# Top-k attention with two gated layers behind it: plain float32 output weights for the first chunk, one bank for rows of two batches, a later start of the W2 conversion

## Chip, cores and metric

The kernel runs on one core of one Trainium2 chip. Its time is the device time of one execution in microseconds (us), lower is better. TensorE is called PE here, VectorE DVE, ScalarE ACT, GpSimd POOL, SyncE SP, as in the profile; the DMAs are issued by SP, in the order of its part of the program.

## The reference

```python
# attention: q, k, v are (4, 8, 576, 64)
scores = matmul(q, k.T) / sqrt(64)
kth    = 32nd largest score of the row
attn   = softmax(where(scores >= kth, scores, -1e9))
x      = (attn @ v) as (2304, 512)
# first layer, weights 512 -> 1536 -> 512
x = (silu(x @ w_gate) * (x @ w_val)) @ w_out
# second layer, weights 512 -> 2048 -> 512
h = x @ w_in
out = (h * cos(h)) @ w2_out
```

The weights come as float64, and the kernel makes float32 of their words itself.

## The kernel before, in words

2304 tokens are 18 tiles of 128 rows. Two tiles are a *chunk* of 256 tokens, so there are nine chunks, 0 to 8. A *unit* is one tile and one head: 16 units make a chunk (four pairs of heads, two tiles, two heads), 144 units in all, in the order chunk, pair, tile, head. In a unit PE multiplies q by the 576 keys into one two-bank PSUM tile `sc` (four matmuls of 288 columns, line 549), ACT copies the scores out (`s`, line 555), DVE runs four MAX8 and three MATCH_REPLACE8 over them (lines 581 and 584) to find the 32 largest, POOL makes the bounds (lines 595, 599), ACT makes the kept exponentials (Prelu at 612, Exp at 623). For two units PE then transposes (645), and multiplies by V (683, 686). A sequence of a batch is 576 rows, four tiles and a half, so tile 4 and tile 13 hold rows of two batches. For their 16 units (eight in chunk 2, eight in chunk 6) `unit_proc` does the scores twice, once with the keys of each batch: it computes all 128 rows, copies the 64 that count, waits until `sc` is free, computes all rows with the other keys, and copies the other 64.

The first layer of a chunk follows one chunk later, in 12 steps f over the 1536 hidden columns, spread between the units of the next chunk: `gemm_proc` multiplies x by W1 (`gv`, line 817, 24 matmuls for each f), ACT and POOL make the gated product `vv`, ACT and POOL split it into two float32r parts `gh` and `gl` (851, 854), and `wout_proc` adds 12 matmuls of 256 columns to `y` (871): high weights by `gh`, high weights by `gl`, low weights by `gh`, for four blocks of output. Both factors are split into a float32r part and its rest.

The output weights `wo` are converted once, in the time of chunk 0's first layer, in 24 half blocks: `convert` is a load (`wr`), three ACT operations (216, 224, 220), one DVE join (261) and one POOL addition (230); `halve` then splits the float32 result with one ACT copy (275) and one POOL subtraction (279). `wo0_store_proc` writes each split block of 512 KB to DRAM (line 336), and `wo_proc` loads it again for each of the eight later chunks (line 368). Two buffers hold `wo` blocks. Early pieces of the second layer's weights W2 go through the same `convert`, 48 of them, and back to DRAM (`w2_early_proc`).

What sets the order: a planner (`Plan`) runs when the program is built, takes a cost for each step and a due time (`due_unit(u)` is u times 4.97), and writes one fixed sequence for each engine and for SP's DMA queue. On the chip every engine works its sequence off in that order and waits where something is not there. The second layer (lines 1080 to 1144) begins when the last chunk's first layer is nearly done.

## Time and profile before

| | |
|---|---|
| time, median of 3 runs | 1313.93 us (1313.81 to 1314.13) |
| the profiled execution's own time | 1311.49 us |
| its span, first to last instruction | 1309.7 us |
| mean granted clock of PE | 0.965 of full speed |
| busy: PE, DVE, ACT, POOL | 92%, 78%, 76%, 51% of the span |
| attention, with the first layer of the chunk before between | until 810.4 us, the end of the last MAX8 |
| second layer alone | the last 402.7 us |

An engine's busy time is the union of its instructions' spans, so a busy PE need not be issuing at its full rate. The rows below give the attention chunk by chunk. Such a stretch begins with the first MAX8 of the chunk's first unit and ends with that of the next chunk.

### The profile page before, as it was taken

The page shows a single profiled execution, that of the slowest core. Times are in us where ns is not written, and L with a number is a line of the kernel's source. Part 1 is how long each engine was busy: PE and PEld are TensorE (multiplying, and loading weights), DVE is VectorE, ACT ScalarE, POOL GpSimd, SP SyncE. Part 2 cuts the span into 40 slices and gives each one's busy share as a digit, 9 for nine tenths or more (in the row PEclk, how much of TensorE's full clock was granted, in tenths as well). Part 3 has the DMA queues.
Part 4 walks back from the last instruction along what each step waited for, and adds up shares of the span by engine and source line. Part 5 has one row for each costly group of instructions (what it writes and reads, how often), then busy time and mean ns, then how long its engine had stood idle before and what let it go on. Part 6 is the DMA issues. An engine that isn't in the chain of part 4 may idle for free.

```text
span 1309.7 us, 25255 instructions
## 1 busy us (share of the span) xinstructions
PE 1205.0 (92%) x8704; PEld 1115.2 (85%) x8704; DVE 1018.0 (78%) x2040; ACT 990.6 (76%) x2308; POOL 668.5 (51%) x1111
## 2 busy tenths in 40 slices
PE   3567789799999999999999999987999999999998
PEld 2356678799999999989999999987899999999997
DVE  7998998899999999988999997336655555555554
ACT  7998899998988988899888887548655545555554
POOL 5865888776678776676767665767210000000000
PEclk9866899999999999999999999998999999999999
DMA  6642244564546654555544432574010100000000
GB/s 216 194 126 78 70 142 166 178 190 154 168 141 184 184 177 147 161 151 188 167 142 156 136 119 89 196 249 160 28 43 7 39 11 26 23 11 27 1 25 25
DMA packets 85408, 153.69 MB, mean 117 GB/s; under 512 B 16416, under 2 KB 39456, under 8 KB 85280
## 3 DMA queue, kind: packets, MB, share of 16 engines
q1 hardware_dynamic: 85280, 152.08, 37.0%
q8 instruction: 68, 1.11, 0.3%
q14 instruction: 60, 0.49, 0.1%
HBM read 130.02 MB, written 22.02 MB: 116 GB/s over the span
## 4 chain that ended last, share of the span: by engine, by line
PE 49%; DVE 6%; ACT 6%; DMA 4%; POOL 3%; issue 2%; SPq 0%; POOLq 0%; ACTq 0%; DVEq 0%
PE o L1144 15%; PE h L1080 14%; PE gv L817 8%; PE y L871 5%; DVE m L581 2%; PE av L686 2%; DVE w L584 2%; PE sc L549 2%; PE tp L645 2%; DMA wr<-in_w 2%; DVE th L844 1%; POOL w L1016 1%; ACT s L555 1%; DMA wo<-wo 1%; PE av L683 1%
## 5 line engine op out<-in xcount | busy, mean ns | idle before, releaser
L817 PE MATMUL gv<-xh,w 128*128 128x256 f32 x1536 | 332.3, 295 | 7.6 <-ACT hg L784 7.5
L581 DVE MAX8 m<-w 128x8 f32<-128x576 f32 x432 | 307.9, 746 | 0.5
L817 PEld LDWEIGHTS gv<-xh,w 128*128 128x128 f32 x1536 | 259.5, 193 | 15.6 <-ACT hg L784 9.8
L817 PE MATMUL gv<-xl,w 128*128 128x256 f32 x768 | 218.1, 284 | 0.0
L584 DVE MATCH_REPLACE8 w<-m,w 128x576 f32<-128x576 f32 x288 | 212.1, 741 | 0.0
L1080 PE MATMUL h<-x2h,w 128*128 128x384 f32 x720 | 200.8, 340 | 4.2 <-DVE g L1114 4.0
L871 PE MATMUL y<-gh,wo 128*128 128x256 f32 x864 | 178.1, 289 | 6.9 <-ACT gh L851 3.6
L1144 PE MATMUL o<-w,gh 128*128 128x512 f32 x540 | 183.8, 395 | 0.0
L549 PE MATMUL sc<-K,q 128*128 128x288 f32 x640 | 131.6, 331 | 39.4 <-ACT s L555 26.6
L871 PEld LDWEIGHTS y<-gh,wo 128*128 128x128 f32 x864 | 144.0, 194 | 10.7 <-ACT gh L851 4.4
L1047 POOL TENSOR_TENSOR x2l<-x,x2h 128x384 fp32r<-128x384 f32 x24 | 25.7, 1070 | 244.3 <-ACT x2h L1036 244.3
L817 PEld LDWEIGHTS gv<-xl,w 128*128 128x128 f32 x768 | 147.9, 193 | 0.0
L549 PEld LDWEIGHTS sc<-K,q 128*128 128x128 f32 x640 | 100.8, 208 | 51.9 <-ACT s L555 26.8
L645 PE MATMUL tp<-ident,e 128*128 128x128 f32 x648 | 116.4, 292 | 30.1 <-ACT pt L650 27.4
L1114 DVE TENSOR_TENSOR g<-r,h 128x384 f32<-128x384 f32 x96 | 53.1, 554 | 116.7 <-ACT r L1109 116.7
L1080 PEld LDWEIGHTS h<-x2h,w 128*128 128x128 f32 x720 | 132.7, 189 | 9.0 <-DVE g L1114 5.1
L1107 ACT ACTIVATE r<-r 128x384 f32<-128x384 f32 x96 | 50.2, 525 | 109.7 <-DVE r L1104 109.7
L854 POOL TENSOR_TENSOR gl<-vv,gh 128x256 fp32r<-128x256 f32 x108 | 81.1, 751 | 95.1 <-ACT gh L851 63.3
L871 PE MATMUL y<-gl,wo 128*128 128x256 f32 x432 | 123.9, 287 | 1.5 <-POOL gl L854 1.3
L1080 PE MATMUL h<-x2l,w 128*128 128x384 f32 x360 | 121.8, 338 | 0.0
L555 ACT ACTIVATE s<-sc 128x576 f32<-128x576 f32 (+1 forms) x160 | 104.1, 651 | 21.9 <-PE sc L549 20.2
L581 DVE MAX8 m<-s 128x8 f32<-128x576 f32 x144 | 105.0, 744 | 17.1 <-ACT s L555 15.5
(109 smaller groups left out, 2955.4 us busy)
## 6 DMA issues: line engine op xcount, KB each, us to landing
wo<-wo SPq DMA_DIRECT2D x108, 512.0 KB, 3.6
w_raw<-in_w SPq DMA_DIRECT2D x24, 512.0 KB, 4.9
V<-in_vP SPq DMA_DIRECT2D x48, 256.0 KB, 2.9
wr<-in_w SPq DMA_DIRECT2D x48, 256.0 KB, 3.7
kx<-in_kT SPq DMA_DIRECT2D x64, 144.0 KB, 2.9
qx<-in_qT SPq DMA_DIRECT2D x70, 128.0 KB, 3.1
wr<-in_wo SPq DMA_DIRECT2D x24, 256.0 KB, 2.8
w2d<-cvx SPq DMA_DIRECT2D x48, 128.0 KB, 3.0
```

The source lines that it names most:

```text
L549: nc.tensor.matmul(sc[:, s, :HALF], q[:, a, t * 128:t * 128 + 128], k[:, s * HALF:s * HALF + HALF], start=a == 0, stop=a == 1)
L555: nc.scalar.activation(st["s"][r0:r1], sc[r0:r1, :, :HALF], AF.Copy)
L581: nc.vector.max(out=st["m"][:, 8 * i:8 * i + 8], in_=st["w"] if i else st["s"])
L584: nc.vector.match_replace(out=st["w"], in_to_replace=st["m"][:, 8 * i:8 * i + 8], in_values=st["w"] if i else st["s"], imm_value=LOWEST)
L645: nc.tensor.transpose(st["ps"][:, j - j0], e[:, j * 128:j * 128 + 128], ident)
L817: nc.tensor.matmul(gv[g], w[kk // 2][:, a, g, kk % 2], m[:, kk], start=kk == 0 and i == 0, stop=kk == KT - 1 and i == 2)
L854: end = yield "POOL", 0.69, lambda: nc.gpsimd.tensor_sub(G[c, f][1], vv, G[c, f][0]), due, True
L871: nc.tensor.matmul(y1p[d // 2][:, d % 2], w[:, a, d * 128:d * 128 + 128], m, start=f == 0 and i == 0 and d % 2 == 0, stop=f == NF1 - 1 and ...
L1080: nc.tensor.matmul(st["h"], w[:, a, kk * 128:kk * 128 + 128], m[:, kk], start=kk == 0 and n == 0, stop=kk == KT - 1 and n == 2)
L1107: yield "ACT", 0.41, lambda: nc.scalar.activation(r, r, AF.Abs), due, True
L1114: nc.vector.tensor_mul(st["g"], r, h)
L1144: nc.tensor.matmul(o[t], a[:, cs], W2[f, 1][:, m], start=f == 0 and n == 0, stop=f == NF2 - 1 and n == 2)
```

## The change

Three edits are made together.

- **Scores of two batches.** `unit_proc` issues the matmuls for both batches one behind the other, the second batch's keys for all 128 rows first, and then the first batch's for the rows 0 to 63 alone, into the same bank. One ACT copy of 128 rows follows. `sc` is freed once for each unit.
- **Chunk 0's output weights.** The POOL addition that ends `convert` writes float32 straight into the `wo` block, and nothing is split: chunk 0's `wout_proc` issues four float32 matmuls for each f (the unsplit weights by the unsplit `vv`) in place of 12 float32r ones, and `gemm_proc` returns for chunk 0 before the split into `gh` and `gl`. The block is stored as 256 KB to a new tensor `wo32`. In chunk 1 `wo_proc` loads those 256 KB, splits them with one ACT copy and one POOL subtraction of 512 columns, and stores the split block of 512 KB to `wo`, from which chunks 2 to 8 load as before. So 24 ACT copies and 24 POOL subtractions of 256 columns, and 12 pairs of `gh` and `gl`, go; 12 copies and 12 subtractions of 512 columns come, and 12 stores move from chunk 0's time to chunk 1's. There are 12 more DMAs in all (120 on `wo` blocks for 108).
- **W2.** The due time of the i-th early piece is `due_unit(46 + 1.9 * i)` and was `due_unit(38 + 2 * i)`.

```diff
@@ -261,7 +262,7 @@
         t = yield "DVE", 0.08 + 0.55 * wide, lambda: nc.vector.scalar_tensor_tensor(
             st["x"], high, 3, st["y"], op0=OP.logical_shift_left, op1=OP.bitwise_or), due, True
         r_cy.free(n, t, plan)
-        t = yield "POOL", 0.13 + 1.12 * wide, lambda: cv_pool(raw, st["x"]), due, True
+        t = yield "POOL", 0.13 + 1.12 * wide, lambda: cv_pool(raw, st["x"], (into or (lambda: st["x"]))()), due, True
         read(t)
 
     def halve(raw, tile_out, due, read, done):
...
@@ -322,19 +324,23 @@
         now = yield "DMA", 1.05, load, due - 4.0, True
         yield r_wo.gate(f)
 
-        def tile_out():
+        def into():
             if f not in WO:
-                WO[f] = moe.tile([128, 2, DM], F32R, tag="wo", name="wo", bufs=r_wo.n)
-            return WO[f][:, :, cs]
-
-        plan.start(halve(st["raw"], tile_out, due, lambda t: r_wr.free(i, t, plan),
-                           lambda t: ev_wo0[f].set(t, plan)), now)
+                WO[f] = moe.tile([128, 2, DM], F32, tag="wo", name="wo", bufs=r_wo.n)
+            return WO[f][:, 0, cs].bitcast(I32)
+
+        def read(t):
+            r_wr.free(i, t, plan)
+            r_cvx.free(st["n"], t, plan)
+            ev_wo0[f].set(t, plan)
+
+        plan.start(convert(st["raw"], due, read, st, into), now)
 
     def wo0_store_proc(f):
         yield ev_wo0[f]
         ev_wo[0, f].set(ev_wo0[f].time, plan)
-        t = yield "DMA", 2.1, lambda: nc.sync.dma_start(wo[f], WO[f].bitcast(F32)), moe_due(0, f), True
-        wo_stored[f].set(t, plan)
+        t = yield "DMA", 1.1, lambda: nc.sync.dma_start(wo32[f], WO[f][:, 0]), moe_due(0, f), True
+        wo_whole[f].set(t, plan)
         r_wo.free(f, t, plan)
 
 
...
@@ -342,7 +348,7 @@
 
     def w2_early_proc(i):
         f, q = divmod(i, 4)
-        due = due_unit(38 + 2 * i)
+        due = due_unit(46 + 1.9 * i)
         cs = slice(q * 256, q * 256 + 256)
         k = 2 * NF1 + i
         yield r_wr.gate(k)
...
@@ -360,15 +366,27 @@
 
     def wo_proc(c, f):
         k = c * NF1 + f
-        yield wo_stored[f]
+        yield wo_whole[f] if c == 1 else wo_stored[f]
         yield r_wo.gate(k)
+        due = moe_due(c, f)
 
         def load():
             WO[k] = moe.tile([128, 2, DM], F32R, tag="wo", name="wo", bufs=r_wo.n)
-            nc.sync.dma_start(WO[k].bitcast(F32), wo[f])
-
-        t = yield "DMA", 1.6, load, moe_due(c, f), True
+            if c == 1:
+                nc.sync.dma_start(WO[k][:, 1].bitcast(F32), wo32[f])
+            else:
+                nc.sync.dma_start(WO[k].bitcast(F32), wo[f])
+
+        t = yield "DMA", 1.1 if c == 1 else 1.6, load, due, True
+        if c == 1:
+            x = WO[k][:, 1].bitcast(F32)
+            yield "ACT", 0.52, lambda: nc.scalar.activation(WO[k][:, 0], x, AF.Copy), due, True
+            t = yield "POOL", 1.25, lambda: nc.gpsimd.tensor_sub(WO[k][:, 1], x, WO[k][:, 0]), due, True
         ev_wo[c, f].set(t, plan)
+        if c == 1:
+            t = yield "DMA", 2.1, lambda: nc.sync.dma_start(wo[f], WO[k].bitcast(F32)), due, True
+            wo_stored[f].set(t, plan)
+            r_wo.free(k, t, plan)
 
 
     K, Q, V = {}, {}, {}
...
@@ -530,7 +548,7 @@
     ev_av = {(c, p): Event(SIZES[c]) for c in range(NCH) for p in range(NP)}
     ev_sum = {(c, p): Event(2 * SIZES[c]) for c in range(NCH) for p in range(NP)}
     r_x, r_rs = Ring(2), Ring(1)
-    tp_count, sc_count = [0], [0]
+    tp_count = [0]
 
     def unit_proc(u):
         c, p, t, h = units[u]
...
@@ -543,29 +561,28 @@
         yield r_s.gate(u + 1)
         q = Q[c, p, h]
 
-        def qk(k):
-            for s in range(2):
-                for a in range(2):
-                    nc.tensor.matmul(sc[:, s, :HALF], q[:, a, t * 128:t * 128 + 128], k[:, s * HALF:s * HALF + HALF],
-                                     start=a == 0, stop=a == 1)
-
-        def copy(r0, r1):
-            if "s" not in st:
-                st["s"] = att.tile([128, 2, HALF], F32, tag="s", name="s", bufs=r_s.n)
-            nc.scalar.activation(st["s"][r0:r1], sc[r0:r1, :, :HALF], AF.Copy)
-
-
+        def qk():
+
+            for b, r0, r1 in segs[::-1]:
+                k = K[b, p, h]
+                for s in range(2):
+                    for a in range(2):
+                        nc.tensor.matmul(sc[:r1, s, :HALF], q[:, a, t * 128:t * 128 + r1],
+                                         k[:, s * HALF:s * HALF + HALF], start=a == 0, stop=a == 1)
+
+        def copy():
+            st["s"] = att.tile([128, 2, HALF], F32, tag="s", name="s", bufs=r_s.n)
+            nc.scalar.activation(st["s"], sc[:, :, :HALF], AF.Copy)
+
+        yield r_sc.gate(u)
+        end = yield "PE", 0.57 * len(segs), qk, due - SC_LEAD, True
         for b, r0, r1 in segs:
-            n = sc_count[0]
-            sc_count[0] += 1
-            yield r_sc.gate(n)
-            end = yield "PE", 0.57, lambda k=K[b, p, h]: qk(k), due - SC_LEAD, True
             if kb_last[b, p, h] == u:
                 r_k.free(kvis[b, p, h], end, plan)
-            if t == SIZES[c] - 1 and r1 == 128:
-                r_q.free((c * NP + p) * 2 + h, end, plan)
-            end = yield "ACT", 0.53, lambda r0=r0, r1=r1: copy(r0, r1), due - SC_LEAD + 1.0, True
-            r_sc.free(n, end, plan)
+        if t == SIZES[c] - 1:
+            r_q.free((c * NP + p) * 2 + h, end, plan)
+        end = yield "ACT", 0.53, copy, due - SC_LEAD + 1.0, True
+        r_sc.free(u, end, plan)
         st["s"] = st["s"].rearrange("p a b -> p (a b)")
         yield r_w.gate(u)
         yield r_m.gate(u)
...
@@ -844,6 +861,10 @@
         yield name, cost, lambda: eng.tensor_mul(th, th, hg), due, True
         end = yield name, cost, lambda: eng.tensor_mul(vv, th, vv), due, True
         r_th.free(k, end, plan)
+        if c == 0:
+            G[c, f] = vv
+            ev_g[c, f].set(end, plan)
+            return
         yield r_g.gate(k)
 
         def hi():
...
@@ -865,16 +886,22 @@
             yield ev_wo[c, f]
 
             def part(d, f=f, k=k):
+                w = WO[k]
+                if c == 0:
+                    nc.tensor.matmul(y1p[d // 2][:, d % 2], w[:, 0, d * 128:d * 128 + 128], G[c, f],
+                                     start=f == 0 and d % 2 == 0, stop=f == NF1 - 1, skip_group_check=True)
+                    return
                 gh, gl = G[c, f]
-                w = WO[k]
                 for i, (a, m) in enumerate(((0, gh), (0, gl), (1, gh))):
                     nc.tensor.matmul(y1p[d // 2][:, d % 2], w[:, a, d * 128:d * 128 + 128], m,
                                      start=f == 0 and i == 0 and d % 2 == 0, stop=f == NF1 - 1 and i == 2,
                                      skip_group_check=True)
 
             for d in range(KT):
-                end = yield "PE", 0.36, lambda d=d, part=part: part(d), due, False
+                end = yield "PE", 0.36 if c else 0.45, lambda d=d, part=part: part(d), due, False
             r_g.free(k, end, plan)
+            if c == 0:
+                r_vv.free(k, end, plan)
             r_wo.free(k, end, plan)
         due = moe_due(c, NF1)
         for d in range(KT):
```

What the planner makes of it, at three places. The names in the rows are the tiles of the program; the lines of the changed kernel are some 17 to 20 higher than before. First ACT near unit 33, one of the eight of chunk 2 with rows of two batches. Before, from the middle of a `convert` on:

```order
L224 ACTIVATE cvx<-wr 128x256
L220 ACTIVATE wr<-wr 128x256
L783 ACTIVATE th<-gv_98 128x256
L784 ACTIVATE hg<-gv_98 128x256
L851 ACTIVATE gh_2648<-vv 128x256
L731 ACTIVATE rs<-tp 128x256
L555 ACTIVATE s<-sc 64x576
L275 ACTIVATE wo<-cvx 128x256
L216 ACTIVATE wr<-wr 128x256
L224 ACTIVATE cvx<-wr 128x256
L220 ACTIVATE wr<-wr 128x256
L555 ACTIVATE s<-sc 64x576
```

and now, from that unit's Prelu on:

```order
L629 ACTIVATE e<-s,b_2417 128x576
L575 ACTIVATE s<-sc 128x576
L217 ACTIVATE wr<-wr 128x256
L225 ACTIVATE cvx<-wr 128x256
L221 ACTIVATE wr<-wr 128x256
L800 ACTIVATE th<-gv_99 128x256
L801 ACTIVATE hg<-gv_99 128x256
L748 ACTIVATE rs<-tp 128x256
L465 ACTIVATE K<-kx 128x576
L756 ACTIVATE rx<-av 128x256
L640 ACTIVATE e,sm<-e,b_2417 128x576
L217 ACTIVATE wr<-wr 128x256
```

The copies of 64 rows and of `wo<-cvx` are gone, and one copy of 128 rows (line 575) stands for two; the conversion's triples are still there. Second PE, where chunk 0 multiplies by its first output weights. Before:

```order
L817 MATMUL gv_98<-xh,w_2_360 128x256
L871 MATMUL y_100<-gh_1309,wo 128x256
L871 MATMUL y_100<-gl_1310,wo 128x256
L871 MATMUL y_100<-gh_1309,wo 128x256 x2
L871 MATMUL y_100<-gl_1310,wo 128x256
L871 MATMUL y_100<-gh_1309,wo 128x256
L871 MATMUL y_101<-gh_1309,wo 128x256
L871 MATMUL y_101<-gl_1310,wo 128x256
L871 MATMUL y_101<-gh_1309,wo 128x256 x2
L871 MATMUL y_101<-gl_1310,wo 128x256
```

and now:

```order
L570 MATMUL sc<-K,q 128x288 x4
L700 MATMUL av<-pt,vtail_106 128x128
L703 MATMUL av<-pt,V 64x128 x8
L891 MATMUL y_101<-vv,wo 128x256 x2
L891 MATMUL y_102<-vv,wo 128x256 x2
```

The twelve matmuls by `gh` and `gl` have become four by `vv`. Third SP's queue in the time of chunk 1's first layer. Before, loads of split blocks (line 368) only:

```order
L368 DMA wo<-wo 128x1024
L515 DMA V<-in_vP 128x512
L517 DMA vtail_104<-in_vP 64x64 x2
L368 DMA wo<-wo 128x1024
L488 DMA qx<-in_qT 64x2x256 x2
L357 DMA w2d<-cvx 128x256
L353 DMA wr<-in_w 128x256
L515 DMA V<-in_vP 128x512
L517 DMA vtail_105<-in_vP 64x64 x2
L368 DMA wo<-wo 128x1024
```

and now loads of whole blocks (line 376) and stores of split ones (line 387):

```order
L376 DMA wo<-wo_65 128x512 x2
L506 DMA qx<-in_qT 64x2x256 x2
L387 DMA wo<-wo 128x1024
L533 DMA V<-in_vP 128x512
L535 DMA vtail_106<-in_vP 64x64 x2
L387 DMA wo<-wo 128x1024
L458 DMA kx<-in_kT 64x576 x2
L376 DMA wo<-wo_65 128x512 x2
L506 DMA qx<-in_qT 64x2x256 x2
L387 DMA wo<-wo 128x1024 x2
L376 DMA wo<-wo_65 128x512
```

Loads and stores of `wo` alternate, and the pieces of W2 (lines 353 and 357 before) have moved behind. On DVE the early W2 pieces' joins stand behind units 38, 40 (two), 42, 44 and 45 in chunk 2 before, and behind units 44 and 47 now; the last stands behind unit 131 before and 134 now.

## Rows read from the trace of the kernel before

**Rows 1.** Busy time in stretches: length, PE, PEld, DVE, ACT, POOL (instructions), clock, DMA share, GB/s.
```profile
104.40:202.40 98.00, 77.58 (x549) 69.44 (x547) 90.77 (x189) 85.83 (x211) 77.83 (x123) 0.83 0.31 103
202.40:305.20 102.80, 91.86 (x805) 85.87 (x805) 90.17 (x180) 95.57 (x240) 79.70 (x137) 0.98 0.58 183
305.20:389.20 84.00, 83.92 (x760) 81.09 (x758) 83.67 (x183) 73.83 (x187) 56.49 (x106) 1.00 0.49 151
389.20:473.30 84.10, 81.52 (x719) 77.86 (x717) 81.56 (x178) 76.07 (x195) 64.61 (x115) 1.00 0.59 180
...
556.40:646.50 90.10, 87.71 (x793) 83.67 (x794) 81.71 (x175) 80.82 (x199) 65.67 (x118) 1.00 0.56 170
646.50:730.60 84.10, 83.42 (x763) 80.34 (x762) 83.16 (x180) 73.45 (x192) 55.19 (x107) 1.00 0.49 150
...
810.40:907.00 96.60, 83.72 (x650) 80.65 (x649) 38.36 (x46) 56.97 (x139) 64.13 (x75) 0.94 0.60 198
907.00:1309.70 402.70, 398.88 (x1988) 359.20 (x1986) 215.71 (x383) 220.95 (x431) 29.48 (x26) 1.00 0.08 25
```

**Rows 2.** Waits, 202.4 to 305.2 us: who for whom, us, times, longest.
```profile
DVE m L581 <- ACT s L555: 5.0, 7, 1.8
DVE cvx L261 <- ACT cvx L224: 4.2, 2, 2.6
```

**Rows 3.** Waits, 556.4 to 646.5 us.
```profile
DVE m L581 <- ACT s L555: 7.0, 2, 4.1
```

**Rows 4.** Timeline around 612 us, chunk 6: start, duration, instruction, idle before it.
```profile
609.77 0.39 PE L683 MATMUL av<-pt,vtail 128*128 128x128 f32 x2
...
612.41 0.28 PE L871 MATMUL y<-gl,wo 128*128 128x256 f32 x1
...
612.53 0.28 PE L871 MATMUL y<-gh,wo 128*128 128x256 f32 x1
...
612.65 0.70 PE L549 MATMUL sc<-K,q 128*128 128x288 f32 x4
...
613.39 0.64 ACT L555 ACTIVATE s<-sc 64x576 f32<-64x576 f32 x1 [0.66 <-PE sc L549]
...
614.70 0.70 PE L549 MATMUL sc<-K,q 128*128 128x288 f32 x4
...
615.88 0.65 ACT L555 ACTIVATE s<-sc 64x576 f32<-64x576 f32 x1
...
616.63 0.76 DVE L581 MAX8 m<-s 128x8 f32<-128x576 f32 x1 [4.10 <-ACT s L555]
```

**Rows 5.** Instructions by line and shape: busy us, mean ns, idle before.
```profile
L555 ACT ACTIVATE s<-sc 64x576 f32<-64x576 f32 x32 | 20.6, 643 | 4.0 <-PE sc L549 3.7
...
L279 POOL TENSOR_TENSOR w<-cvx,w 128x512 fp32r<-128x512 f32 x24 | 30.6, 1278 | 8.9 <-ACT w L275 8.5
...
L275 ACT ACTIVATE w<-cvx 128x512 fp32r<-128x512 f32 x24 | 14.9, 626 | 1.0 <-POOL cvx L230 0.9
```

**Rows 6.** Stretches, tile `wo` alone: length, PE, PEld, ACT, POOL.
```profile
104.40:202.40 98.00, 9.69 (x72) 9.11 (x72) 5.41 (x13) 9.59 (x13) 0.83 0.31 103
202.40:305.20 102.80, 22.45 (x156) 20.58 (x156) 4.56 (x11) 8.26 (x11) 0.98 0.58 183
```

**Rows 7.** Stretches, tile `gh` alone: length, PE, PEld, DVE, ACT, POOL.
```profile
104.40:202.40 98.00, 9.69 (x48) 7.96 (x48) 0.00 (x0) 2.98 (x7) 5.17 (x7) 0.83 0.31 103
202.40:305.20 102.80, 22.21 (x104) 17.80 (x104) 0.00 (x0) 5.08 (x12) 8.83 (x12) 0.98 0.58 183
```

**Rows 8.** Stretches, tile `wr` alone: length, DVE, ACT, POOL.
```profile
202.40:305.20 102.80, 11.29 (x16) 20.64 (x51) 12.39 (x17) 0.98 0.58 183
305.20:389.20 84.00, 3.21 (x8) 8.91 (x21) 5.23 (x7) 1.00 0.49 151
```

**Rows 9.** The page, DMA issues: KB each, median us to landing.
```profile
wo<-wo SPq DMA_DIRECT2D x108, 512.0 KB, 3.6
...
wr<-in_wo SPq DMA_DIRECT2D x24, 256.0 KB, 2.8
```

More of the change, by code (lines that the diff above doesn't have):

```diff
@@ L162, in topk_attention_moe_moe @@
     wo = dram.tile([NF1, 128, 2, DM], F32, name="wo")
+    wo32 = dram.tile([NF1, 128, DM], F32, name="wo32")
     w2d = dram.tile([NS2, 128, 2 * DM], F32, name="w2d")
@@ L227, in cv_join, with cv_pool @@
         nc.vector.scalar_tensor_tensor(x, cv_words(raw)[1], 3, y, op0=OP.logical_shift_left, op1=OP.bitwise_or)
-    def cv_pool(raw, x):
-        nc.gpsimd.tensor_tensor(x, x, cv_words(raw)[0], op=OP.add)
+    def cv_pool(raw, x, out):
+        nc.gpsimd.tensor_tensor(out, x, cv_words(raw)[0], op=OP.add)
     W1, WO = {}, {}
@@ L238, in topk_attention_moe_moe, with convert @@
     cv_count = [0]
-    for f in range(NF1):
+    for f in range(2 * NF1):
         r_wo.freed[f] = Event(2)
-    def convert(raw, due, read, st):
+    def convert(raw, due, read, st, into=None):
         low, high = cv_words(raw)
@@ L308, in topk_attention_moe_moe @@
     ev_wo0 = [Event(2) for _ in range(NF1)]
+    wo_whole = [Event() for _ in range(NF1)]
     def wo0_proc(i):
@@ L994, in w2_proc @@
             r_cy2.free(n, t, plan)
-            t = yield "POOL", 1.23, lambda: cv_pool(st["raw"], st["x"]), due, True
+            t = yield "POOL", 1.23, lambda: cv_pool(st["raw"], st["x"], st["x"]), due, True
             r_raw2.free(n, t, plan)
```

## The prediction

> **What bounds the kernel now.** I read the table of stretches first, chunk by chunk, then who waits for whom in the two stretches that stand out, and then the timeline of one such wait. Chunks 3, 4 and 7 take 84.0, 84.1 and 84.1 us for their 16 units, and DVE and PE are both busy for 97 to 100% of that [rows 1]. That is what 16 units cost when all goes well. Three stretches are longer: chunk 1, which I call A, with 98.0 us, chunk 2, which I call B, with 102.8, and chunk 6 with 90.1 [rows 1]. In B DVE is busy 90.2 us and PE 91.9 of 102.8, so neither of the two is full there; ACT is, with 95.6 us or 93%, where chunk 3 asks 73.8 of it [rows 1]. DVE waits in B for the score copies (5.0 us in 7 waits) and for the second ACT step of the conversions (4.2 us in 2) [rows 2]. In chunk 6 two waits of DVE for score copies make 7.0 us [rows 3], and the timeline shows how the longer one comes about: a copy of 64 rows ends at 614.03, PE issues the second batch's matmuls behind other work at 614.70, the second copy comes at 615.88, and MAX8 starts 4.10 us late [rows 4]. Behind the attention come 96.6 us of the last chunk's first layer and 402.7 us of the second layer alone, in which PE is busy 398.9 [rows 1]. The change does not reach into that; what the attention saves moves it forward as a whole, since each engine's sequence there hangs on the last chunk's x.
>
> **The change part by part.** A and B hold all of chunk 0's first layer: 13 and 11 of the 24 `wo` copies [rows 6], 7 and 5 of chunk 0's 12 `gh` (the 12 of B hold chunk 1's first 7) [rows 7].
>
> *ACT in A.* 13 `wo` copies (5.41 us) and 7 `gh` (2.98) go: 85.8 becomes 77.4. POOL loses 9.59 and 5.17: 77.8 becomes 63.1 [rows 1, 6, 7].
>
> *ACT in B.* Eight copies of 64 rows go (8 x 0.643 = 5.1) [rows 5], 11 `wo` copies (4.6) [rows 6] and five of twelve `gh` (2.1) [rows 7]. Four W2 pieces leave B, as DVE's order shows (six joins behind units 32 to 47 before, two now); 17 pieces took 20.64 us of ACT, so four take 4.9 [rows 8]. Ten of the twelve new copies of 512 columns stand there by ACT's order; the same form is the split of W1, 0.626 us each, so 6.3 come [rows 5]. Net: 95.6 - 5.1 - 4.6 - 2.1 - 4.9 + 6.3 = 85.2. POOL: 79.7 - 8.3 - 3.7 - 2.9 + 9 x 1.278 = 76.3 [rows 1, 5 to 8], well under B's length.
>
> *What that makes of the lengths.* Three bounds for B. ACT at today's share of 93% would need 85.2 / 0.93 = 91.6. DVE has four joins fewer at 11.29 / 16 = 0.71 [rows 8], so 87.4, and at the share of chunk 3 87.7. PE: chunk 6 has the same two-batch units and nearly the same count of matmuls (793 for 805), and was busy 87.7 [rows 1]; with a half of the extra below, 89.6. The longest of the three holds: B goes from 102.8 to 91.6, 11.2 less. A is bound by DVE: 90.8 busy, at chunk 3's share 91.1, and ACT at its present 87.6% would need 88.4. I put A at 92, 6.0 less. In chunk 6 the eight removed copies take away the second trip; PE, busy 87.7, is the bound, so 88.0, 2.1 less [rows 1].
>
> *What comes later.* Four W2 pieces now fall behind B. DVE is full there, so their joins count in full: 4 x 3.21 / 8 = 1.6 us more [rows 8]. Their ACT steps, and two new copies and three subtractions in chunk 3, lie beside DVE: ACT has 10 us free there and POOL 27 [rows 1]; without that cover ACT's 4.9 and these 5.1 us [rows 5] would come on top.
>
> *Plain float32 matmuls.* The trace has no 256-column one. The nearest row is line 683: one float32 matmul of 128 columns is two records, 0.39 us together where one record is 0.28 [rows 4], so 0.11 apart, 0.22 for 128 columns and 0.44 for 256. Three float32r ones of 256 take 3 x 0.12 = 0.36, from the starts at 612.41, 612.53 and 612.65 [rows 4]. 48 of them make 48 x 0.08 = 3.8 us more. Bounds: two records of 256 columns at 0.12 each would be 5.8 us less, and at half the clock the difference doubles to 7.7 us more. I take 3.8 us, since line 683 is the same kind of matmul. It lies in A and B, where PE has 20.4 and 10.9 us free [rows 1], so it costs nothing as long as PE does not become the bound.
>
> *Costs that I put at nothing.* The buffer `vv` is held until the matmuls instead of until `gl`; two stand ready. The extra 12 DMAs and the moved stores: the DMA share is 0.31 in A and 0.58 in B [rows 1]. What SP waits for is the third rival. Sum: -11.2 - 6.0 - 2.1 + 1.6 = -17.7. The profiled execution took 1311.5 (span 1309.7), the median of the runs is 1313.9, 2.4 above it, and I keep that distance: 1313.9 - 17.7 = 1296.2.
>
> **A rule that speaks against it.** DVE's joins read two tensors. They last 3.21 / 8 = 0.40 us in chunk 3 and 0.71 in B [rows 8], where POOL is busy 78% of the time and not 67% [rows 1]. The Trainium skill, in "SBUF — State Buffer", section "SBUF: two separate sides", says that a DVE operation with two SBUF inputs and a GpSimd operation that reads SBUF exclude each other for a whole instruction; by that rule the new wide subtractions hold DVE's joins off for longer than the halves did, and the longer joins of B agree with it. By the rows, such a subtraction lasts 1.278 us [rows 5]; behind units 36 to 47, where they stand, DVE has three joins left. Even if each met one in full, 3 x 1.28 = 3.8 us come on top, and the sum is -13.9. The joins beside them read 0.71 already, so I leave this out of the sum.
>
> **The rivals.** *First, PE binds.* If PE is the bound in A and B, since the plain matmuls come where its clock is half (the mean granted clock of A is 0.83 [rows 1]), their 7.7 us count in full, and with the blocked joins 3.8 more: -17.7 + 7.7 = -10.0 to -6.2, some 1304 to 1308. For it speaks that PE is full in every good chunk; against it the 31 us that it has free in A and B.
>
> *Second, only the copies help.* ACT's relief could be worth nothing, if what delays A and B is the chain from chunk to chunk and not ACT's load. Then DVE's waits for copies go (5.0 in B [rows 2], 2.1 in chunk 6) and the joins come: -5.5, so 1308.4. Against it: in B ACT is at 93%.
>
> *Third, slower: the round trip of `wo` blocks in chunk 1.* Two buffers, and by SP's order a pair of loads waits until the pair before is stored. The trip is a load of 2.8 [rows 9], a copy of 0.63, two subtractions of 1.28 [rows 5] and the store's 3.6 [rows 9]: 9.6 us for two f. A chunk has six such pairs, and 84.0 / 6 = 14.0 us for each [rows 1]. If the copy, the subtractions and SP's entries come late in their queues by more than 4.4 us in a pair, chunk 1's output matmuls wait on PE, and the scores queued behind them there, and so DVE. Each further us costs 6. The gain is used up at 4.4 + 17.7 / 6 = 7.4 us of lateness; at 9 us the change costs 6 x 4.6 - 17.7 = 9.9, so 1324. For it: SP's loads stand behind those of q, k and V, each of which waits for a buffer too. Against it: the trip before had the same two buffers, a longer conversion and the same store.
>
> *Fourth, deeper.* If all waits and the lengthened joins go, A falls to its DVE work of 90.8 [rows 1], B to 90.2 - 11.3 + 12 x 0.40 = 83.7 [rows 1, 8], and chunk 6 to the 84.0 of a good chunk: -7.2 - 19.1 - 6.1 + 1.6 = -30.8, 1283.1.
>
> That the change does not do what it says can be excluded for the counts, which the order shows, though not for the time.
>
> **How the numbers follow.** The forecast, 1288 to 1304 (its own range), gets 0.55; deeper, 1281 to 1288, 0.12; PE or the joins bind, 1304 to 1308, 0.13; only the copies, about 1308, 0.08; no difference 0.04; the round trip 0.08. The range of 8 in 10 is 1283 to 1309. A difference of 0.2% or 2.6 us is about what a measurement can tell from none. Faster by more: 0.55 + 0.12 + 0.13 + 0.07 = 0.87; within: 0.05; slower: 0.08.
>
> **What would show it.** The stretch of chunk 2 should be 89 to 94 us, with ACT busy about 85; chunk 1's 90 to 94; chunk 6's 87 to 89, without a wait of 3 to 4 us for a copy; chunks 3, 4 and 7 84 to 85, and the stretch behind the attention as long as before. The plain matmuls should stand 0.4 to 0.5 us apart at full clock. The prediction is wrong if B stays near 100 with ACT under 85% (then the second rival), if PE waits for `wo` in chunk 1's matmuls (the third), or if the joins in B grow beyond 0.8 us (the rule).

## The result, and the profile after

The changed kernel takes 1283.58 us (median of 4 runs, 1282.05 to 1284.8) where the kernel before took 1314.03 (median of 4 runs, 1313.81 to 1314.48): a ratio of 0.9769, 95% interval 0.9748 to 0.979. The profiled execution took 1282.05 us, its span is 1280.3. The forecast was 1296.2 with a range of 1283 to 1309, so the time lies at the range's lower edge, where the fourth rival ("deeper", 1283.1) stood. The median is 0.6 us inside the range and one of the four runs lies outside it.

The table of stretches of the changed kernel, cut at the same instructions as [rows 1]: length, busy time of PE, PEld, DVE, ACT and POOL (instructions), clock, DMA share, GB/s. The nine chunks, then all that follows the last MAX8.

```profile
11.20:100.40 89.20, 48.78 (x219) 36.80 (x220) 87.73 (x181) 84.27 (x169) 65.38 (x85) 0.71 0.54 171
100.40:194.80 94.40, 81.71 (x594) 71.60 (x594) 90.33 (x192) 87.25 (x212) 67.59 (x108) 0.92 0.35 106
194.80:280.60 85.80, 83.24 (x740) 79.26 (x739) 84.89 (x181) 79.07 (x197) 70.63 (x120) 1.00 0.57 178
280.60:362.60 82.00, 81.69 (x743) 79.12 (x742) 82.00 (x179) 74.23 (x189) 61.29 (x111) 1.00 0.58 181
362.60:444.30 81.70, 79.24 (x695) 75.13 (x694) 79.45 (x169) 73.36 (x187) 63.85 (x113) 1.00 0.61 181
444.30:530.70 86.40, 86.36 (x772) 83.24 (x771) 86.11 (x188) 77.29 (x197) 61.26 (x116) 1.00 0.53 163
530.70:612.10 81.40, 79.97 (x723) 76.62 (x722) 78.99 (x170) 71.19 (x180) 62.68 (x113) 1.00 0.57 175
612.10:699.30 87.20, 86.69 (x796) 83.65 (x795) 86.04 (x185) 78.17 (x201) 59.44 (x114) 1.00 0.50 155
...
780.90:1280.30 499.40, 484.68 (x2660) 440.43 (x2655) 251.68 (x428) 279.25 (x572) 96.36 (x102) 0.99 0.18 59
```

Against [rows 1], chunk 1 (A) went from 98.0 to 94.4 and chunk 2 (B) from 102.8 to 85.8. What follows the attention takes 499.4 us in this execution (96.6 + 402.7 before), so all of the gain lies in the attention. In B, DVE is now busy 84.89 of 85.8 us: it has become the engine that is full, and ACT's share is 79.07 / 85.8 = 92%. For chunk 0, which the rows ahead of the prediction don't show, the same view of the kernel before gives 93.2 us:

```profile
11.20:104.40 93.20, 51.98 (x242) 39.06 (x240) 89.75 (x184) 87.14 (x174) 66.01 (x86) 0.79 0.54 169
```

The waits of DVE in chunk 2 of the changed kernel (who for whom, us, times, longest):

```profile
DVE cvx L262 <- POOL K L469: 0.5, 1, 0.5
DVE sm L724 <- ACT e L640: 0.3, 1, 0.3
DVE cvx L262 <- issue: 0.2, 1, 0.2
```

Before, the same view had two more lines beside those of [rows 2]:

```profile
DVE cvx L261 <- POOL rs L743: 1.6, 1, 1.6
DVE cvx L261 <- issue: 1.0, 2, 0.5
```

In chunk 6 of the changed kernel, which answers to [rows 3]:

```profile
DVE m L598 <- ACT s L575: 1.2, 1, 1.2
DVE m L598 <- POOL th L859: 1.1, 1, 1.1
```

The waits of DVE in B, 9.2 us in [rows 2] and 11.8 with these two lines, are down to 1.0, and the 7.0 us for two score copies in chunk 6 to 1.2 for one. The timeline of a unit with rows of two batches in chunk 6 shows the merged form (start, duration, instruction): eight matmuls one behind the other, then one copy.

```profile
531.56 1.22 PE L570 MATMUL sc<-K,q 128*128 128x288 f32 x8
...
533.83 0.63 ACT L575 ACTIVATE s<-sc 128x576 f32<-128x576 f32 x1
```

The plain float32 matmuls, from the timeline of PE in chunk 1: four of them are eight records.

```profile
152.12 1.89 PE L891 MATMUL y<-vv,wo 128*128 128x256 f32 x8
```

A single record lasts 0.38 us, so the eight start (1.89 - 0.38) / 7 = 0.216 apart, 0.431 for each matmul at a granted clock of 1.00, where 0.44 was estimated. The split in chunk 1, in the table of instructions by shape (busy us, mean ns, idle before), has nearly the price that was taken from W1's split (0.626 and 1.278):

```profile
L384 POOL TENSOR_TENSOR wo<-wo 128x512 fp32r<-128x512 f32 x12 | 15.6, 1298 | 2.4 <-ACT wo L383 1.2 <-PE av L703 1.0
...
L383 ACT ACTIVATE wo<-wo 128x512 fp32r<-128x512 f32 x12 | 7.7, 644 | 0.5 <-DMA wo<-wo 0.5
```

### The profile page after: what moved, and what is told of

Same layout as the page of the kernel before. It is cut to its first block, busy times and chain, and to the rows that moved or that the text cites. A ratio compares the mean times of both kernels' runs of the same rounds, so it can differ in the third digit from the quotient of the medians.

```text
span 1280.3 us, 25083 instructions
## 1 busy us (share of the span) xinstructions
PE 1195.2 (93%) x8656; PEld 1105.5 (86%) x8656; DVE 1011.7 (79%) x2040; ACT 977.2 (76%) x2268; POOL 661.9 (52%) x1087
## 4 chain that ended last, share of the span: by engine, by line
PE 64%; ACT 15%; DMA 7%; DVE 6%; issue 4%; POOL 3%; SPq 1%; POOLq 0%; ACTq 0%; DVEq 0%
PE o L1171 15%; PE h L1107 15%; PE gv L834 12%; PE y L896 8%; PE av L703 4%; PE sc L570 4%; PE tp L662 3%; DVE m L598 2%; DVE w L601 2%; ACT e L640 2%; DMA wo<-wo 2%; ACT e L629 2%; DMA wr<-in_w 2%; ACT pt L667 2%; ACT s L575 1%
## 5 line engine op out<-in xcount | busy, mean ns | idle before, releaser
L834 PE MATMUL gv<-xh,w 128*128 128x256 f32 x1536 | 328.5, 293 | 3.3 <-ACT hg L801 2.5
L834 PEld LDWEIGHTS gv<-xh,w 128*128 128x128 f32 x1536 | 256.4, 190 | 9.8 <-issue 4.5
L896 PE MATMUL y<-gh,wo 128*128 128x256 f32 x768 | 158.2, 289 | 4.5 <-DMA wo<-wo 3.4
L570 PE MATMUL sc<-K,q 128*128 128x288 f32 (+1 forms) x640 | 125.7, 325 | 27.9 <-DVE K L446 10.0
L896 PEld LDWEIGHTS y<-gh,wo 128*128 128x128 f32 x768 | 127.2, 193 | 9.2 <-issue 5.0
L570 PEld LDWEIGHTS sc<-K,q 128*128 128x128 f32 (+1 forms) x640 | 97.5, 199 | 37.0 <-POOL K L469 9.3
L667 ACT ACTIVATE pt<-tp 128x512 f32<-128x512 f32 (+1 forms) x216 | 106.3, 492 | 16.8 <-PE tp L662 14.9
L1171 PEld LDWEIGHTS o<-w,gh 128*128 128x128 f32 x540 | 101.4, 188 | 19.6
L640 ACT ACTIVATE e<-e,b 128x576 f32<-128x576 f32 x144 | 112.5, 781 | 3.0 <-POOL b L616 0.6
L662 PEld LDWEIGHTS tp<-ident,e 128*128 128x128 f32 x648 | 81.9, 148 | 36.1 <-ACT pt L667 34.0
```

The lines of the kernel that those rows point to most:

```text
L570: nc.tensor.matmul(sc[:r1, s, :HALF], q[:, a, t * 128:t * 128 + r1], k[:, s * HALF:s * HALF + HALF], start=a == 0, stop=a == 1)
L640: nc.scalar.activation(st["e"], st["e"], AF.Exp, bias=st["b"][:, 2:3], scale=1.0, accum_out=smT[c, p][:, j:j + 1])
L662: nc.tensor.transpose(st["ps"][:, j - j0], e[:, j * 128:j * 128 + 128], ident)
L667: lambda: nc.scalar.activation(ptT[c, p, t][:, j0:j1], st["ps"][:, :j1 - j0], AF.Copy),
L834: nc.tensor.matmul(gv[g], w[kk // 2][:, a, g, kk % 2], m[:, kk], start=kk == 0 and i == 0, stop=kk == KT - 1 and i == 2)
L896: nc.tensor.matmul(y1p[d // 2][:, d % 2], w[:, a, d * 128:d * 128 + 128], m, start=f == 0 and i == 0 and d % 2 == 0, stop=f == NF1 - 1 and ...
```

## The experiments

Three theories were put to the test. Theory 1: ACT's load decides A and B, and what was taken off ACT is what was gained. Theory 2: the second trip through the score bank in units of two batches was the main cost. Theory 3: the planner's new order moves the time by some us whatever the edit.

**Each edit alone, and in pairs.** The six kernels are the changed one or the one before with some of the hunks. Merged scores only (`unit_proc` of the change in the kernel before):

```diff
...
+        yield r_sc.gate(u)
+        end = yield "PE", 0.57 * len(segs), qk, due - SC_LEAD, True
...
+        end = yield "ACT", 0.53, copy, due - SC_LEAD + 1.0, True
+        r_sc.free(u, end, plan)
```

> Only the merged score matmuls and copies, in the kernel before. Theory 1 (the load of ACT and POOL around chunk 0's output weights holds up chunks 1 and 2, and the second trip through the score banks is a smaller part): 6 to 9 us less than before, about 1306, chunk 6 near 85 us and chunk 2 near 98. Theory 2 (the second trip is the main thing, in chunk 2 as in chunk 6): 20 us less, about 1294, with chunk 2 near 88.

Plain weights only (all hunks of the change but those of `unit_proc` and `w2_early_proc`):

```diff
...
+        if c == 0:
+            G[c, f] = vv
+            ev_g[c, f].set(end, plan)
+            return
...
```

> Only the plain float32 weights in chunk 0 and their split in chunk 1. Theory 1: 10 to 14 us less, about 1302, gained in chunks 1 and 2, chunk 6 as before at 90 us. Theory 2: at most 4 us less, about 1310, since the second trip is still there.

W2 only:

```diff
-        due = due_unit(38 + 2 * i)
+        due = due_unit(46 + 1.9 * i)
```

> Only the later start of the W2 pieces. Theory 1: four pieces less in chunk 2 relieve ACT there by 4.9 us, so 3 to 5 us less, about 1310. Theory 2: within 2 us of before, about 1314. If what matters is only how the planner happens to arrange the work, any of these three could move by 5 us either way, in stretches that the edit does not touch.

The changed kernel without merged scores:

```diff
...
-        end = yield "PE", 0.57 * len(segs), qk, due - SC_LEAD, True
...
-        end = yield "ACT", 0.53, copy, due - SC_LEAD + 1.0, True
...
+            yield r_sc.gate(n)
+            end = yield "PE", 0.57, lambda k=K[b, p, h]: qk(k), due - SC_LEAD, True
...
+            end = yield "ACT", 0.53, lambda r0=r0, r1=r1: copy(r0, r1), due - SC_LEAD + 1.0, True
...
```

> The changed kernel with the second trip through the score banks put back. Theory 1: most of the gain stays in chunk 2, 15 to 20 us less than before, about 1296, and chunk 6 is back at 90 us. Theory 2: the gain is mostly gone, about 1308.

The changed kernel with the old start of W2:

```diff
-        due = due_unit(46 + 1.9 * i)
+        due = due_unit(38 + 2 * i)
```

> Plain weights and merged copies, W2's conversion as before the change (38 + 2.0 i). Alone, plain weights gave -18 us, merged copies and W2's start nothing net, all three -30. Theory A (the first two edits free VectorE and W2's start is worth nothing): 1281 to 1287 us, chunk 2 at 85 to 88 us, VectorE idle in the nine chunks near 13 us. Theory B (W2's later start is what lets the other two pay in chunk 2, since 13 instead of 10 W2 pieces fall there): 1290 to 1297 us, chunk 2 at 90 us or more.

The changed kernel with the output weights of before:

```diff
...
-        if c == 0:
-            G[c, f] = vv
-            ev_g[c, f].set(end, plan)
-            return
...
```

> Merged copies and W2's start, output weights split in chunk 0 as before the change. Theory A (edits add up, each of these two alone gave 0): 1309 to 1315 us. Theory C (copies pay 15 us whenever W2 starts at unit 46, which is what separates the changed kernel from the one without merged copies): 1295 to 1300 us, with chunk 2 under 92 us.

Measured: the median of the runs with its ratio to the kernel before on the same chip, and from the table of stretches of each profiled execution the lengths in us (3 to 8 are the six chunks together, attention is chunks 0 to 8, rest what follows the last MAX8). The kernel before, run beside them, had medians of 1312.76 us (19 runs) for the three single edits and for plain weights with W2, and 1313.98 (8 runs) for the other two pairs; the first line has its runs beside the changed kernel.

| edits | time | ratio (95%) | chunk 0 | A | B | 3 to 8 | attention | rest |
|---|---|---|---|---|---|---|---|---|
| none | 1314.03 | | 93.2 | 98.0 | 102.8 | 505.2 | 799.2 | 499.3 |
| merged scores | 1312.41 | 0.9995 (0.9974 to 1.0015) | 89.2 | 92.8 | 97.3 | 507.9 | 787.2 | 507.5 |
| plain weights | 1294.5 | 0.9859 (0.9834 to 0.9885) | 92.4 | 93.0 | 94.9 | 502.5 | 782.8 | 498.4 |
| W2 | 1312.97 | 0.9998 (0.9982 to 1.0014) | 93.1 | 100.2 | 103.7 | 506.8 | 803.8 | 498.2 |
| plain, W2 | 1299.04 | 0.9883 (0.9858 to 0.9909) | 93.1 | 92.5 | 95.6 | 507.6 | 788.8 | 498.0 |
| merged, plain | 1297.34 | 0.9879 (0.9856 to 0.9902) | 88.8 | 94.3 | 87.1 | 503.8 | 774.0 | 508.1 |
| merged, W2 | 1307.59 | 0.9945 (0.992 to 0.9971) | 88.8 | 94.6 | 95.6 | 504.8 | 783.8 | 508.0 |
| all three | 1283.58 | 0.9769 (0.9748 to 0.979) | 89.2 | 94.4 | 85.8 | 500.3 | 769.7 | 499.4 |

The times alone look like three edits that do little one by one and much together. The stretches show two separate things. Within the attention the plain weights give 13 to 16 us beside whatever else is there (799.2 to 782.8, 787.2 to 774.0, 803.8 to 788.8, 783.8 to 769.7), and the merged scores 9 to 20 (12.0 alone, 8.8 beside plain weights, 20.0 and 19.1 beside W2). W2's start costs 5 to 6 without merged scores and saves 3 to 4 with them. Behind the attention there are two lengths, 498 to 499 and 507 to 508. The three kernels with merged scores and not all three edits have the longer one. So the merged scores alone gained 12.0 in the attention of their profiled execution and lost 8.2 behind it. That execution (1307.71 us) is one of the fastest of ten; the median, 1312.41, shows no gain at all, so the stretches explain most of the missing 12 us and not the last 4.

Of the expectations, that of Theory 1 for the plain weights came nearest: 18.3 us less where 10 to 14 were expected, 12.9 of the attention's 16.4 in A and B. The merged scores alone met chunk 2 (97.3 for about 98), but neither total, and chunk 6 took 89.0 and not 85. W2 alone stayed where Theory 2 had it. Without the merged scores 13.7 us of gain were left and not 15 to 20, and chunk 6 took 84.4 and not 90, so the second trip by itself does not make that chunk long. The last two pairs met none of their theories as a whole: merged and plain had the chunk 2 of one (87.1) with a total beyond the other (1297.34), merged and W2 lay between (1307.59, chunk 2 at 95.6).

One part of the longer one is seen in the waits of PE, in the first 115 us behind the last MAX8. With merged scores and plain weights:

```profile
PE y L896 <- ACT gh L872: 4.6, 3, 3.6
PE gvl L834 <- ACT hg L801: 4.5, 2, 3.5
PE y L896 <- POOL gl L875: 4.0, 7, 1.1
```

and with all three edits:

```profile
PE y L896 <- DMA wo<-wo: 2.4, 1, 2.4
PE h L1107 <- DVE g L1141: 2.3, 1, 2.3
PE gvl L834 <- ACT hg L801: 2.2, 2, 1.4
PE y L896 <- POOL gl L875: 1.9, 4, 0.5
```

With two edits PE waits once for 3.6 and once for 3.5 us, and the table of stretches shows the granted clock around these waits, 10 us each:

```profile
825.10:835.10 10.00, 6.75 (x35) 6.75 (x36) 3.36 (x4) 4.77 (x12) 4.91 (x6) 0.66 0.59 198
875.10:885.10 10.00, 5.26 (x30) 4.64 (x29) 6.65 (x10) 7.96 (x16) 7.90 (x8) 0.84 0.32 109
885.10:895.10 10.00, 9.23 (x37) 8.61 (x37) 5.74 (x9) 8.76 (x17) 4.95 (x4) 0.65 0.52 149
```

A mean of 0.65 says that PE ran a good part of these 10 us at 1.2 GHz and not 2.4, in or behind stretches in which it was busy 6.75 and 5.26 us of 10. In the changed kernel the lowest 10 us there have 0.83. Over the 115 us PE is idle for 14.4 us with two edits and 10.8 with three, at a mean clock of 0.93 and 0.97; 3.6 us of idle time and some 115 x 0.04 = 4.6 us of clock (an estimate) make up most of the 8.7 between the two. The kernel before, however, has a wait of 4.0 us and a still lower clock behind its attention, and yet the shorter length:

```profile
900.40:910.40 10.00, 5.98 (x24) 5.56 (x24) 6.96 (x11) 9.18 (x20) 4.26 (x4) 0.59 0.47 151
...
810.40:1309.70 499.30, 482.60 (x2636) 439.85 (x2634) 254.07 (x428) 277.93 (x569) 93.61 (x101) 0.98 0.18 59
```

against this line of merged scores and plain weights:

```profile
785.10:1293.20 508.10, 489.42 (x2666) 444.58 (x2664) 253.00 (x428) 280.59 (x574) 96.09 (x101) 0.98 0.18 59
```

So a part of the 8 to 9 us against the kernel before is work put off: the three kernels of the longer length have 2666 matmul records behind the attention where the kernel before has 2636. The changed kernel has 2660 and the shorter length, so the records do not decide either. That the order which the planner happens to write for this part makes the difference fits all eight kernels, but it is argued from them and was not taken apart further.

**ACT's time against the second trip.** One copy of 128 rows becomes two of 64 in the changed kernel, in the same planned order:

```diff
-            nc.scalar.activation(st["s"], sc[:, :, :HALF], AF.Copy)
+            for b, r0, r1 in segs:
+                nc.scalar.activation(st["s"][r0:r1], sc[r0:r1, :, :HALF], AF.Copy)
```

> The changed kernel, but where a tile holds rows of two batches the one copy of 128 rows is issued as two of 64 rows, in the same planned order: ScalarE gets back some 8 x 0.64 = 5.1 us in chunk 2 and as much in chunk 6 (79.1 -> 84.3 and 71.2 -> 76.3 busy), and no second trip through the bank. Theory 1 of the prediction (ScalarE holds chunk 2 at a share of 93%): chunk 2 becomes 84.3 / 0.93 = 90.6 us, the total 1288 to 1290. Theory 2 (the second trip through the score banks was what cost, ScalarE has room at 92%): chunk 2 stays within 1 us of 85.8, chunk 6 of 81.4, total 1282 to 1285.

1291.49 us (1290.94 to 1292.03), 0.9828 (0.9811 to 0.9845), 7.9 above the changed kernel. Its stretches of chunk 2 and chunk 6:

```profile
195.60:285.90 90.30, 85.59 (x740) 80.60 (x739) 84.33 (x182) 84.35 (x206) 71.43 (x121) 0.98 0.54 169
...
537.30:623.30 86.00, 80.83 (x717) 76.03 (x716) 80.00 (x171) 76.19 (x184) 62.16 (x112) 1.00 0.54 165
```

ACT rises by 5.3 and 5.0 us, the chunks by 4.5 and 4.6, and ACT's share of chunk 2 is 84.35 / 90.3 = 93%. Theory 1 put chunk 2 at 90.6; Theory 2, by which it should have stayed, falls for this part: of the 19.1 us that merged scores save beside the other two edits, 11.2 of the attention come back with the second copies alone, 9.1 of them in chunks 2 and 6. The other 8 are the second trip and the order together. A second copy also lengthens the way from the scores to DVE; the next run looks at that.

The same load behind DVE's work instead of before it:

```diff
-            nc.scalar.activation(st["e"], st["s"], AF.Prelu, bias=st["b"][:, 1:2], scale=SCALE, alpha=STEEP)
+            for b, r0, r1 in segs:
+                nc.scalar.activation(st["e"], st["s"], AF.Prelu, bias=st["b"][:, 1:2], scale=SCALE, alpha=STEEP)
```

> The changed kernel, but the first pass over the scores after the selection (the Prelu into e, 0.78 us) is issued twice in the 16 units whose tile holds two batches; the second writes the same values, planned order as in the changed kernel. ScalarE gets 8 x 0.78 = 6.2 us in chunk 2 and as much in chunk 6, behind VectorE's work of the unit and not between the scores and it. If the 4.4 us that the two-copies run lost in each of those chunks are ScalarE's time (chunk 2 at a ScalarE share of 93 to 94%): chunk 2 becomes (79.1 + 6.2) / 0.935 = 91 us, chunk 6 loses 3 to 5 us, the total 1290 to 1294. If they were the longer way from the scores to VectorE: chunk 2 stays under 87 us, the total 1282 to 1286.

1287.63 us (1286.11 to 1290.43), 0.9804 (0.9782 to 0.9826), between the two expectations. Chunks 2 and 6:

```profile
196.40:285.10 88.70, 84.61 (x733) 79.79 (x731) 84.46 (x181) 82.56 (x198) 69.34 (x118) 0.98 0.55 172
...
537.30:621.70 84.40, 80.21 (x725) 76.83 (x725) 79.25 (x170) 75.74 (x188) 62.42 (x113) 1.00 0.55 169
```

Chunk 2 grew by 2.9 and chunk 6 by 3.0. In chunk 2 ACT rose by 3.5 and not by 6.2, since work of the chunk slipped into the next one (ACT in chunk 3 is 76.36 for 74.23). Its share is again 93%. The stretches come from the slowest of the four runs, so the 2.9 and 3.0 are rather too large than too small. Added ACT time is paid for even where no score copy is made longer, though at about half of its length; how much of the 4.5 us with two copies was the longer way to DVE stays open.

**PE's time.** The plain matmuls of f = 1, 3, 5, 7 and 9 left out:

```diff
+                    if f % 2 and f < NF1 - 1:
+                        return
```

> The changed kernel without the output multiplications of five of the first chunk's twelve weight tiles (40 of its 96 plain matmuls are left out, so the sum of the first chunk lacks them), all else in the same planned order: TensorE has 40 x 0.43 = 17 us less to do over chunk 1 and the start of chunk 2. If TensorE binds there (the first rival of the prediction): 8 to 17 us faster, 1267 to 1276. If VectorE sets those chunks and TensorE's work is hidden: within 2 us of 1283.6, with TensorE's busy time in chunk 1 down from 81.7 to about 65 to 70.

1282.15 us (1281.09 to 1284.52), 0.9759 (0.974 to 0.9779). The expectation took records for matmuls: 40 records are 20 matmuls, so 8.6 us go and not 17. Chunks 1 and 2:

```profile
99.90:194.90 95.00, 77.67 (x578) 68.36 (x577) 90.80 (x192) 87.31 (x213) 67.82 (x108) 0.91 0.34 106
194.90:280.00 85.10, 79.67 (x718) 75.70 (x717) 84.90 (x182) 78.85 (x196) 70.35 (x120) 1.00 0.57 180
```

PE lost 4.0 and 3.6 us of busy time, and the two chunks together changed from 180.2 to 180.1. PE does not bind in A and B.

**The halves `gh` and `gl` of chunk 0 back,** unread:

```diff
...
+            def extra():
+                spare.extend(moe.tile([128, CH], F32R, tag=f"g{a}1", name=f"g{a}1", bufs=r_g.n) for a in "hl")
+                nc.scalar.activation(spare[0], vv, AF.Copy)
+
+            yield "ACT", 0.31, extra, due, True
+            t = yield "POOL", 0.69, lambda: nc.gpsimd.tensor_sub(spare[1], vv, spare[0]), due, True
...
```

> The changed kernel, but ScalarE and GpSimd again make the two halves gh and gl of the first chunk's gated values, which nothing reads: 12 x 0.42 = 5.1 us of ScalarE and 12 x 0.73 = 8.8 us of GpSimd over chunk 1 and the start of chunk 2; the weights stay unsplit and the multiplications plain. Theory 1 (ScalarE's time counts at once in chunk 1, busy 87.2 of 94.4): chunk 1 and 2 together 4 to 6 us longer, total 1287 to 1290. If it is only the halves of the weights, their store of 2.1 us and the way through DRAM that held chunk 1: within 2 us of 1283.6.

1290.04 us (1286.49 to 1296.0), 0.9825 (0.9792 to 0.9858). The total is Theory 1's, the place is not: in the profiled execution (1286.49) chunks 1 and 2 take 92.9 and 85.9, which is 1.4 less than in the changed kernel, and chunks 3 to 8 take 505.1 for 500.3. The planner knew these steps and laid the rest round them, so the run does not show which chunk pays. What part of A's gain is `gh` and what the halves of the weights stays open.

**W2's start.** Two neighbours of 46:

```diff
-        due = due_unit(46 + 1.9 * i)
+        due = due_unit(50 + 1.9 * i)
```

> The changed kernel with W2's conversion from unit 50 instead of 46. Theory 1 (ScalarE's time in chunk 2): fewer of its pieces in chunk 2, but VectorE is busy 84.9 of 85.8 us there, so at most 1 us less in chunk 2 and the work comes back in chunks 3 to 8; attention 768 to 773 us. Theory 3 (the planned order of the first 100 us after the attention decides 8 to 9 us): total either 1281 to 1286 or 1290 to 1294.

and the same with 42:

> The changed kernel with W2's conversion from unit 42 instead of 46: two more of its pieces in chunk 2, at 3 ScalarE steps of 0.44 us and a join of 0.65 us each. Theory 1: chunk 2 longer by 2 to 4 us, attention 771 to 774 us (with 38 + 2.0 i it was 774.0). Theory 3: the stretch after the attention is 498 to 500 or 507 to 508 us, so the total 1284 to 1288 or 1293 to 1297.

50 gives 1292.62 us (1292.38 to 1296.15), 0.9848 (0.9822 to 0.9874); 42 gives 1287.73 (1284.25 to 1289.43), 0.9799 (0.9775 to 0.9823). B is 84.9 and 86.8 with ACT at 77.34 and 79.39: the right way in both, though 42 costs B 1.0 us and not 2 to 4. The attention is 777.2 and 773.5, and the rest, 502.1 and 501.1, lies between the two lengths that were expected. The 777.2 were not expected either: with 50 the chunks 3 to 8 take 509.2 for 500.3, far more than B can save, where DVE has 0.9 us of idle time left. Of the starts tried (38, 42, 46, 50; 38 with a step of 2) 46 is the best, and no version here beats the changed kernel by more than its runs scatter while doing all of the work.

## Why the prediction was right, and where it was off

The sum had four terms: B -11.2, A -6.0, chunk 6 -2.1, later joins +1.6. Measured in the profiled executions: B -17.0, A -3.6, chunk 0 -4.0, chunks 5 to 7 together -2.3 (257.3 to 255.0), chunks 3, 4 and 8 together -2.6 (247.9 to 245.3), and the rest +0.1: 29.4 in all for 17.7. The time lies inside the range, but by luck as much as by the sum: 6.6 of the 29.4 us came from chunks 0, 3, 4 and 8, for which the sum had no gain. Of the stretches that were named as signs, that behind the attention came (499.4 for 499.3) and A missed by little (94.4 for 90 to 94). B (85.8 for 89 to 94), chunk 6 (81.4 for 87 to 89) and chunks 3, 4 and 7 (82.0, 81.7 and 87.2 for 84 to 85) lie outside. The plain matmuls came as named.

*B: the mechanism was right, ACT's sum was too large.* The step was "ACT at today's share of 93% would need 85.2 / 0.93 = 91.6". The share holds well: 93% before, 92% after, 93% in both runs with added ACT time, and where two copies brought ACT to 84.35 the chunk came to 90.3. Over the kernels of the table it runs from 90% (85.75 of 95.6, merged scores and W2) to 95% (90.04 of 94.9, plain weights), so a length from it is good to some 3 us. ACT's need was not 85.2 but 79.07, and 79.07 / 0.93 = 85.0, for 85.8 measured; as DVE was busy 84.89 of it, this one length alone can't tell which of the two set it. The tile `wr` in chunks 1 to 3 of the changed kernel (length, DVE, ACT, POOL) shows the largest piece:

```profile
100.40:194.80 94.40, 7.51 (x16) 19.39 (x48) 11.94 (x16) 0.92 0.35 106
194.80:280.60 85.80, 6.48 (x10) 13.14 (x32) 6.71 (x9) 1.00 0.57 178
280.60:362.60 82.00, 3.86 (x8) 10.21 (x25) 5.99 (x8) 1.00 0.58 181
```

The conversions in B fell by 7.5 us of ACT (20.64 in [rows 8]) where four W2 pieces, 4.9, were counted. The loads for that tile which SP issued in B tell the two kinds apart, before and after (count, shortest, median and longest in ns, first and last start):

```profile
L320 SPq DMA_DIRECT2D wr<-in_wo x9: 328/334/687, 203.0 to 233.9; - x9
L353 SPq DMA_DIRECT2D wr<-in_w x8: 328/376/592, 237.1 to 299.9; - x8
...
L322 SPq DMA_DIRECT2D wr<-in_wo x6: 328/333/334, 198.5 to 214.9; - x6
L359 SPq DMA_DIRECT2D wr<-in_w x3: 417/445/530, 218.2 to 270.8; - x3
```

Three pieces of `wo` left B besides five of W2. By the same views of the other kernels, W2's start alone moves nothing (nine and eight loads, 20.60 us of ACT), plain weights alone take 3.3 us (six and seven, 17.30), merged scores alone 0.7 (nine and seven, 19.90), plain weights with W2 7.8 (seven and four, 12.82) and merged scores with W2 4.7 (nine and five, 15.90). So the plain weights, for which no such term was in the sum, let the conversions of `wo` end sooner, and the later start of W2 shows only beside one of the other edits. Eight and not ten new copies of 512 columns stood in B, 5.16 for 6.3 us. The score copies (15.45 to 10.15) and `gh` (5.08 to 2.97) came out as summed. These pieces make 3.9 of the 6.1 us between 85.2 and 79.07; the rest lies in steps of the units and of the first layer that fell outside B. DVE, at 84.89 busy of 85.8, was then nearly full, which the fourth rival had at 83.7.

*A: 3.6 of the 6.0 us came.* DVE's 90.33 us of work are as counted (90.8). ACT did not fall to 77.4 but stayed at 87.25: conversions that left B are done here (48 ACT steps on `wr`, 19.39 us, for 42 and 16.95 before), and the chunk holds more of its neighbours' work (24 copies of `pt` for 22, 17 score copies for 16). A is 2.4 longer than the 92 put down, and the waits of DVE in it show one on ACT of that size:

```profile
DVE cvx L262 <- ACT gv L225: 2.6, 1, 2.6
```


*Chunk 6: the bound was not one.* "PE, busy 87.7, is the bound" failed: the chunk takes 81.4 with PE busy 79.97, since 70 matmul records fewer lie in it (723 for 793) and its neighbours hold more (772 and 796 for 738 and 763). PE works off one sequence, so its busy time in a chunk says what fell there and not what the chunk needs. The three together gained 2.3, near the term of 2.1, and this too is partly luck: merged scores take 2.0 us from the three alone and 5.0 beside the other two edits, and W2's start by itself adds 2.1. The Trainium skill, in "Perfetto Trace Analysis", section "Identifying the Most-Contended Engine", says that the share of time in which matmuls are shown busy is no good measure for how near TensorE is to its limit. This case agrees: in B of the changed kernel PE is shown busy for 83.24 of 85.8 us, 97%, and 3.6 us less of its work there and 4.0 less in A changed the sum of the two by 0.1.

*Chunk 0, which the prediction left out.* It takes 88.8 to 89.2 us in all four kernels with merged scores of the table and 92.4 to 93.2 in the four without. It holds no tile of two batches; what changes there is the order, since `sc` is now given out by unit number: the program writes chunk 0's scores for the units 0, 2, 1, 3, 4, 6, 5, 7 and so on before, and in the order of their numbers now. PE has 219 matmul records in it and not 242. About half of the 4.0 us is DVE's idle time (3.5 to 1.5); the other half is busy time of DVE (89.75 to 87.73), of which one MAX8 and one MATCH_REPLACE8 of the last unit now fall behind the cut, into A. The prediction took an edit for a local one that changes a rule of the planner everywhere.

*The joins.* In B they last 6.48 / 10 = 0.65 us for 0.71 before, with POOL busy 82% for 78%; in chunk 3 they rose from 0.40 to 3.86 / 8 = 0.48, with POOL at 75% for 67%. The rule of the Trainium skill in "SBUF — State Buffer", section "SBUF: two separate sides", by which the new wide subtractions should have held them off for longer, has chunk 3 on its side and not B; its 3.8 us did not come. Nor did the 1.6 us for the joins behind B: chunks 3 to 8 take 4.9 us less in all.

*The rivals.* The first (PE binds) falls by the matmuls left out. The second (only the copies help) falls by the plain weights alone, whose kernel is 18.3 us faster than the one before. The third (the round trip of `wo`) did not happen: in A and B the view of PE's waits names none for `wo`, chunk 3, into which chunk 1's last weights reach, has one of 0.3 us, and the one of 2.4 us shown above comes behind the attention. The fourth came in its total, by other parts: B 85.8 for 83.7, A 94.4 for 90.8, and chunk 0 and the order of the later chunks gave what these two lacked.

## What to carry to other kernels

Where one written order drives all engines, take a stretch's length from the engine whose added time is paid for there, and check the sum of that engine's work over the neighbouring stretches too: work that leaves one stretch turns up in another, and the busy time of an engine in a stretch is what fell there, not what the stretch needs. Judge an edit by the stretch that it touches and by what follows it apart: here 12 us were gained in one part and 8 lost in another, and the total read "no difference". An edit to how a buffer is given out is an edit to the whole order.

## What the runs showed of the hardware

A plain float32 matmul of 256 columns is two records and takes 0.431 us at a granted clock of 1.00, where a float32r one takes 0.12 [rows 4]; four of them, 1.72 us, replace twelve of 1.44. PE has seven waits of 3.4 to 4.0 us behind the attention in the kernel before and the three of the longer length; in or behind six of them a stretch of 10 us had a granted clock of 0.59 to 0.67, behind one 0.83, so PE lost more by them than the waits themselves. Runs of the kernel before lay between 1307.13 and 1317.8 us (19 runs), 1310.59 and 1316.27 (8), 1310.45 and 1315.8 (7) and 1313.81 and 1314.48 (4), so that differences of a few us between single profiled executions, W2's start above all, carry little weight.
